# New sort keys for attention work, and fp32 logit products for the last units, in a fused attention and mixture-of-experts kernel

## The chip, the cores and the metric

The kernel runs on one core of a Trainium2 chip. The metric is the device time of one execution in microseconds. Engines are called PE or TensorE (matrix products), DVE or VectorE, ACT or ScalarE, POOL or GpSimd, and SP, which issues most of the DMAs; each works off its own instructions in the order in which the program gives them.

## The reference

Inputs are q, k and v of 8 batches x 8 heads x 576 rows x 64, a gate of 512 x 8, and the weights of 8 experts. Per batch and head:

```
q_d, k_d, v_d = means over groups of 4 rows               # 144 rows
out_up = repeat(softmax(q_d k_d^T / 8) v_d, 4)             # attention over groups
out_local = softmax(where(|i - j| < 4, q k^T / 8, -1e9)) v # a band of 7 keys
x = (out_up + out_local), as 4608 tokens x 512
logits = x @ w_gate                                        # 4608 x 8
# all (token, expert) pairs in order of falling logit; each token goes to the first
# expert that has room; an expert holds 4608 / 8 = 576 tokens
out[token] = relu(x[token] @ w1[e]) @ w2[e]
```

All of it is computed in fp32 or in pairs of f16 parts (a high and a low part), since the order of the logits decides the experts.

## The kernel before, in words

The attention stage comes first, then a routing step for the first expert, then eight experts in turn, each beside the routing of the next. The change touches the attention stage alone.

Tokens are taken in 36 units of 128 (`u`), each made of four windows of 32 queries with 38 keys. A batch (`b`) is 4.5 units long. A unit goes through steps: `s0`, `s1` (local scores on PE, maximum and subtraction on DVE, exponential on ACT; `loc_s`), `t` (four transposes on PE, line 552, copied by ACT as `pt`, line 563), `v0`, `v1` (products with the v rows `vw`, line 574, and normalisation on DVE), `up`/`um`/`add` (the attention over groups is added: up to unit 26 from a product, on DVE; from unit 27 on loaded from DRAM and added by POOL, line 582), `st` (store to DRAM), `lt` (transposes, line 592, and conversion to f16 high parts on ACT, line 601, and low parts on DVE, line 602), `lm` (products with the gate, lines 617 and 620; the logits are written by line 622).

A batch needs fill work: `trw`, `trt` (transposes of its q and k, lines 327 and 340, each copied from PSUM to SBUF by ACT or DVE, `evac`: every fifth copy goes to DVE later on, every second one at first), `gsum`, `gsum_v` (sums over groups of four, lines 267 to 303, on POOL, for batch 0's k on DVE) and `down_s`, `down_t`, `down_v` (the attention over groups, lines 349 to 443).

The order is set by one list. Every step has a key in units of time of one unit, and the list is sorted by it:

```
for j, (name, lag) in enumerate(LOC.items()):
    at = u + lag
    if lag >= 2.0:
        at = u + 2.0 + (lag - 2.0) * (1.0 - CE * max(u - UE, 0)) + max(E0 - u * E1, 0.0)
    if u >= UL:
        at += {"t": TX, "v": VX, "v0": VX, "v1": VX}.get(name, 0.0)
work.sort(key=lambda z: z[:3])
```

Fill work is spread over a stretch (`TW` and `TWS` for the transposes, `DW` and `DWS` for the attention over groups), loads have keys of their own (`LD1` for batch 1, `NEXT` for the later ones, `VWT0` up to unit `UV` and `VWT` from there for `vw`), and so have batch 0's sums (`SUM0`). The engines get their instructions in this order. Some parts of a step are put off by a number of TensorE steps: the exponential of the local scores by `FL` of them, or until `t` of its unit needs it, the low part of `lt` by `FT`. A load whose key is above `PACE0` is paced: SP issues it when the DVE instruction that stands last before it in the list is done; SP takes its DMAs in order.

Units from `UF` on convert the transposed rows as fp32 (line 597) and take four fp32 products instead of eight f16 ones (line 613); before, `UF` is 36, so no unit does.

Of the kernel before, what the change touches and what calls it, by code (L numbers as in the profile page):

```python
# [37 lines left out]
LU = 2  # L38
LA = 3
LT = 5  # L40
NEXT = (("q0", 1.46), ("q1", 1.71), ("k0", 2.06), ("k1", 2.37), ("t", 2.77), ("q2", 3.07), ("q3", 3.38), ("k2", 3.68), ("k3", 4.31),
        ("v0", 4.61), ("v1", 4.77), ("v2", 4.92), ("v3", 5.11), ("w", 5.13))
VWS = 0.22
PACE0 = 0.6
FD = 4
FN = 1
FH = 2
FL = 4
FT = 3
PEL = ("s0", "s1", "t", "v0", "v1", "lt", "lm")  # L50
TW = (0.23, 2.44)
DW = (0.15, 1.9)
DWS = {0: (1.95, 3.56), 7: (0.89, 2.3)}
LOC = {'up': 2.07, 'um': 4.42, 'st': 4.6, 't': 1.194, 'lm': 8.317, 's0': 0.33, 's1': 0.331, 'lt': 5.433, 'v0': 1.842, 'v1': 1.843, 'add': 4.425}
GS1 = ''
GS0 = 'k'
GW = 2
# [11 lines left out]
SETUP = {24: 0, 35: 25}  # L69
SPACE = 0.365  # L70
GS = 32.0
VWT = 1.219
VWT0 = 1.68
UV = 5
T0 = (-0.12, 0.19)
LD0 = (-1.79, -1.53, -1.57, -0.7, 0.51)
LD1 = (-0.99, -0.95, -0.9, -0.89, -0.88, -0.6, -0.55, -0.3, -0.25, 0.2, 0.4, 0.6, 0.8, 2.0)
TWS = {1: (1.54, 2.38)}
E0 = 0.72
E1 = 0.55  # L80
UE = 33
CE = 0.14
UF = 36
UL = 30
TX = 0.0
VX = 0.0
NWARM = 13
EV0 = (0,1)
EN0 = 24
TB = 3  # L90
SUM0 = (0.65, 1.38, 1.73)


def key0(w):
# [7 lines left out]
class Attention:  # L102
# [413 lines left out]
    def loc_s(self, u, g):  # L516
# [18 lines left out]
        if g == 0:  # L535
# [7 lines left out]
                                mx[..., None].to_broadcast([128, 2, 4, KW]), op=OP.subtract)  # L543
        self.after(FL, lambda: nc.scalar.activation(t[:, :, :KW], t[:, :, :KW], AF.Exp, scale=0.125), ("l", u))

# [41 lines left out]
    def log_t(self, u):  # L587
# [6 lines left out]
        pf = p.rearrange("p c t -> p (c t)")  # L594
        if u >= UF:
            xt = xt.rearrange("p a c t -> p (a c t)").bitcast(F32)
# [9 lines left out]
    def log_m(self, u):  # L606
# [3 lines left out]
        l = self.ps.tile([128, 2, E], F32, name="g", bufs=NG)  # L610
        if u >= UF:
            for c in range(4):
# [33 lines left out]
    def run(self, after, ready):  # L646
# [14 lines left out]
        for b in range(B):  # L661
# [5 lines left out]
            else:  # L667
                spread(-2.0, -1.0, t[:2] + t[3:])
                spread(T0[0], T0[1], t[2:3])
                for c in range(2):  # L670
                    for w in "kq":
                        other.append((SUM0[c], lambda w=w, c=c: self.gsum(0, w, 2 * c)))
                other.append((SUM0[2], lambda: self.gsum_v(0)))
            dw = DWS.get(b, DW)
            spread(u0 + dw[0], u0 + dw[1], self.down(b))
            end.append(u0 + dw[1])
            if b + 1 < B:
                for i, (w, at) in enumerate(NEXT):
                    at = max(up + at + (SH1 if b == 1 else 0), -1.0) if b else LD1[i]
                    f = lambda b=b, w=w: self.load_nat(b + 1, w[0], int(w[1]) if w[1:] else None)  # L680
# [18 lines left out]
        for u in range(NT):  # L699
            if u > 1:  # L700
                for c in range(4):
                    at = max(u - (VWT0 if u < UV else VWT) + VWS * c, u - 3.999 + LOC["v0"])
                    f = lambda u=u, c=c: self.load_vw(u, (c,))
                    work.append((at, 0, 0, (lambda f=f: self.paced(f)) if at > PACE0 else f, False))
# [7 lines that stand above are left out]
                if name == "up":  # L712
# [779 lines left out]
```

## Time and profile before

| | us |
|---|---|
| median of three runs | 710.55 |
| lowest and highest | 707.21, 711.26 |
| the profiled execution | 709.79 |
| its span | 708.1 |
| PE busy | 649.8 (92%) |
| DVE busy | 533.6 (75%) |
| ACT busy | 337.7 (48%) |
| POOL busy | 232.7 (33%) |

The span is the stretch from the first to the last instruction of the profiled execution; all places below are counted in us from its start. The profile gives for each engine the time in which an instruction ran, and for each idle stretch what seems to have ended it. [...]

### The profile page before, as it was taken

The page shows a single profiled execution, that of the slowest core. Times are in us where ns is not written, and L with a number is a line of the kernel's source. Part 1 is how long each engine was busy: PE and PEld are TensorE (multiplying, and loading weights), DVE is VectorE, ACT ScalarE, POOL GpSimd, SP SyncE. Part 2 cuts the span into 40 slices and gives each one's busy share as a digit, 9 for nine tenths or more (in the row PEclk, how much of TensorE's full clock was granted, in tenths as well). Part 3 has the DMA queues.
Part 4 walks back from the last instruction along what each step waited for, and adds up shares of the span by engine and source line. Part 5 has one row for each costly group of instructions (what it writes and reads, how often), then busy time and mean ns, then how long its engine had stood idle before and what let it go on. Part 6 is the DMA issues. An engine that isn't in the chain of part 4 may idle for free.

```text
span 708.1 us, 21934 instructions
## 1 busy us (share of the span) xinstructions
PE 649.8 (92%) x8938; PEld 451.0 (64%) x8938; DVE 533.6 (75%) x1562; ACT 337.7 (48%) x650; POOL 232.7 (33%) x303
## 2 busy tenths in 40 slices
PE   6888999889999845999999999999999999999994
PEld 4667878778787733774574575575674674755741
DVE  5798889987989977887889697797797876634500
ACT  4567778787785521532532443443444424424410
POOL 4865374644737420402402303204104106202011
PEclk9899999999999975999999999999999999999997
DMA  9967859777785632605507617638348269814001
GB/s 263 245 157 218 227 159 245 205 205 202 197 238 160 192 117 89 218 1 181 192 1 283 157 43 269 129 116 229 95 183 204 55 233 198 313 35 100 1 31 38
DMA packets 132157, 113.73 MB, mean 161 GB/s; under 512 B 81240, under 2 KB 109912, under 8 KB 132056
## 3 DMA queue, kind: packets, MB, share of 16 engines
q1 hardware_dynamic: 124760, 90.76, 45.0%
q0 software_dynamic: 6432, 20.98, 9.5%
q8 instruction: 71, 1.16, 0.7%
q10 hardware_dynamic: 864, 0.58, 0.3%
q14 instruction: 30, 0.25, 0.1%
HBM read 85.74 MB, written 19.46 MB: 149 GB/s over the span
## 4 chain that ended last, share of the span: by engine, by line
PE 45%; DVE 22%; issue 17%; ACT 5%; DMA 5%; POOL 4%; SPq 1%; ACTq 0%; POOLq 0%; DVEq 0%
PE pH L1279 13%; PE pX L1320 11%; PE g L574 3%; PE pR L871 2%; DVE wl L1202 2%; PE g L327 2%; POOL out_dram L1330 2%; DVE x L453 2%; PE g L552 2%; PE g L592 2%; PE s L532 1%; DVE qt L311 1%; POOL xg L1217 1%; PE g L407 1%; PE pH L1186 1%
## 5 line engine op out<-in xcount | busy, mean ns | idle before, releaser
L1279 PE MATMUL pH<-xt,wh 128*128 128x256 f16 (+1 forms) x1024 | 191.3, 286 | 1.2 <-ACT xt L1238 0.5
L1320 PE MATMUL pX<-wh,ht 128*128 128x512 f16 (+1 forms) x640 | 178.0, 379 | 0.0
L1279 PE MATMUL pH<-xt,wl 128*128 128x320 f16 (+1 forms) x512 | 144.6, 286 | 0.0
L1320 PEld LDWEIGHTS <-ht 128*128 128x128 f16 (+1 forms) x960 | 82.6, 100 | 93.9 <-issue 3.8
L1320 PE MATMUL pX<-wl,ht 128*128 128x512 f16 (+1 forms) x320 | 117.6, 379 | 0.0
L1279 PEld LDWEIGHTS <-wh 128*128 128x128 f16 x1024 | 97.5, 98 | 30.2 <-issue 5.7
L1330 POOL DMA_INDIRECT out_dram<-y,idx x40 | 43.0, 1074 | 177.8 <-ACT y L1327 153.5
L1303 ACT ACTIVATE ht<-pH 128x512 f16<-128x512 f32 (+1 forms) x128 | 45.5, 407 | 112.5 <-PE pH L1279 112.5
L1202 DVE SCALAR_TENSOR_TENSOR wl<-nat,wh 128x512 f16<-128x512 f32 x128 | 83.5, 687 | 14.9 <-ACT wh L1200 8.3
L1327 ACT ACTIVATE y<-pX 128x512 f32<-128x512 f32 (+1 forms) x40 | 23.8, 594 | 103.4 <-PE pX L1320 54.3
L1306 DVE SCALAR_TENSOR_TENSOR ht<-pH,ht 128x512 f16<-128x512 f32 (+1 forms) x128 | 52.3, 450 | 24.4 <-ACT ht L1303 23.9
L1200 ACT ACTIVATE wh<-nat 128x1024 f16<-128x1024 f32 x64 | 67.3, 1053 | 4.1 <-DMA nat<-in_moe_w_dram 4.1
L1217 POOL DMA_INDIRECT xg<-x_dram,idx x40 | 42.5, 1062 | 61.9 <-DVE used L1100 33.4
L1279 PEld LDWEIGHTS <-wl 128*128 128x128 f16 x512 | 49.9, 98 | 12.7 <-issue 0.8
L563 ACT COPY pt<-g 64x512 f32<-64x512 f32 x72 | 41.8, 581 | 28.8 <-PE g L552 27.8
L574 PE MATMUL g<-vw,pt 128*64 128x65 f32 x1152 | 45.5, 229 | 5.6 <-issue 2.7
L574 PEld LDWEIGHTS g<-vw,pt 128*64 128x64 f32 x1152 | 39.6, 142 | 12.7 <-issue 6.6
L327 PE MATMUL g<-ident,nat 128*128 128x128 f32 x256 | 40.4, 283 | 3.9 <-DMA nat<-in_q_dram 3.3
L313 ACT COPY kt<-g 64x512 f32<-64x512 f32 (+1 forms) x60 | 38.3, 639 | 6.2 <-PE g L327 5.2
L1246 DVE SCALAR_TENSOR_TENSOR xs<-xg,xs 128x512 f16<-128x512 f32 (+1 forms) x30 | 20.3, 688 | 26.8 <-ACT xs L1245 15.7
L1019 POOL MEMSET f<- 128x1 bf16 x8 | 0.8, 106 | 116.3 <-DVE sumf L925 44.2
L300 POOL TENSOR_TENSOR gtmp<-kt 128x576 f32<-128x576 f32 x14 | 16.1, 1147 | 61.4 <-ACT kt L313 43.6
(221 smaller groups left out, 1153.0 us busy)
## 6 DMA issues: line engine op xcount, KB each, us to landing
nat<-in_moe_w_dram SPq DMA_DIRECT2D x28, 1024.0 KB
vw<-in_v_dram SPq DMA_DIRECT2D x136, 78.0 KB
x_dram<-x SPq DMA_DIRECT2D x36, 256.0 KB
nat<-in_q_dram SPq DMA_DIRECT2D x32, 256.0 KB
nat<-in_k_dram SPq DMA_DIRECT2D x32, 256.0 KB
nat<-in_v_dram SPq DMA_DIRECT2D x28, 256.0 KB
up<-up_dram SPq DMA_DIRECT2D x9, 256.0 KB
nat<-in_moe_w_dram SPq DMA_DIRECT2D x4, 512.0 KB
```

The costliest lines, as they stand in the source:

```text
L313: self.nc.scalar.copy(out, in_)
L327: nc.tensor.transpose(p[:, a, :, fp], src[:, 4 * hh + 2 * a + s, 2 * fp:2 * fp + 2].rearrange("p f d -> p (f d)"), self.ident)
L563: self.nc.scalar.copy(out, in_)
L574: nc.tensor.matmul(o[64 * i:64 * i + 64, 65 * h:65 * h + 65], pt[:, 2 * (h % 2) + i, 2 * g + h // 2].rearrange("p b q -> p (b q)"), self.v ...
L1200: nc.scalar.activation(hi, r, AF.Copy, scale=sc)
L1202: nc.vector.scalar_tensor_tensor(lo[:, a:a + LOP], r[:, a:a + LOP], sc, hi[:, a:a + LOP], op0=OP.mult, op1=OP.subtract)
L1217: self.fetched = nc.gpsimd.indirect_dma_start(out=xg[:n], out_offset=None, in_=self.x, in_offset=bass.IndirectOffsetOnAxis(ap=idx[:n, c:c ...
L1279: mm = nc.tensor.matmul(p[:, s, :s1 - s0], w[d][a][:, 128 * f:128 * f + 128], xt[:, b, d, s0:s1], start=j == 0, stop=j == len(seq) - 1)
L1303: last = nc.scalar.activation(hi, q, AF.Relu)
L1306: low = nc.vector.scalar_tensor_tensor(lo, q, 0.0, hi, op0=OP.max, op1=OP.subtract)
L1320: mm = nc.tensor.matmul(p[o:o + m], ht[:, f, h0:h0 + m], w[4 + f // 2][b][:, 512 * (f % 2):512 * (f % 2) + 512], start=j < parts, stop=j > ...
L1330: i = nc.gpsimd.indirect_dma_start(out=self.out, in_=y[:n], in_offset=None, out_offset=bass.IndirectOffsetOnAxis(ap=idx[:n, c:c + 1], axis=0))
```

## The change

Only constants change. `SUM0` gives the places of batch 0's sums (first half, second half, v), `LOC['t']` that of the local transposes, `FL` the delay of the exponential, `VX` with `UL` an offset of the local values of the last units, `CE` a stretch of the last units' steps, `UF` the first unit with fp32 logits; the others are places of loads.

```
-NEXT = (... ("k1", 2.37), ("t", 2.77), ("q2", 3.07), ... ("v2", 4.92), ("v3", 5.11), ("w", 5.13))
+NEXT = (... ("k1", 2.37), ("t", 3.25), ("q2", 3.07), ... ("v2", 4.92), ("v3", 5.49), ("w", 4.9))
-FL = 4
+FL = 5
-LOC = {..., 't': 1.194, 'lm': 8.317, ...}
+LOC = {..., 't': 1.298, 'lm': 8.317, ...}
-VWT = 1.219
+VWT = 1.154
-UV = 5
+UV = 6
-LD1 = (-0.99, -0.95, -0.9, -0.89, -0.88, -0.6, -0.55, -0.3, -0.25, 0.2, 0.4, 0.6, 0.8, 2.0)
+LD1 = (-0.99, -0.95, -0.9, -0.89, -0.88, -0.87, -0.77, -0.11, -0.25, 0.2, 0.4, 0.6, 0.8, 2.0)
-CE = 0.14
-UF = 36
-UL = 30
+CE = -0.021
+UF = 34
+UL = 31
-VX = 0.0
+VX = -0.052
-SUM0 = (0.65, 1.38, 1.73)
+SUM0 = (0.53, 1.65, 1.67)
```

The step that `UF` switches, in `log_m`:

```
        if u >= UF:
            for c in range(4):
                nc.tensor.matmul(l[:, 0], xt[:, c], self.wgf[:, c], start=c == 0, stop=c == 3)
            nc.vector.tensor_copy(self.lg[:, u], l[:, 0])
            return
```

## Rows read from the trace of the kernel before

**Rows 1.** Busy time of the engines in a stretch, with granted clock and DMA share.

```profile
120.00:140.00 20.00, 17.98 (x550) 15.41 (x542) 18.96 (x56) 13.62 (x26) 13.79 (x21) 1.00 0.78 204
```

**Rows 2.** Groups by line, PE, 60 to 220 us: busy, mean ns, idle before, releasers.

```profile
L552 PE MATMUL g<-ident,sw 128*128 128x128 f32 x100 | 15.8, 281 | 8.0 <-ACT sw L544 7.8
```

**Rows 3.** Waits over the whole span: us in total, times, longest.

```profile
PEld g L327 <- DMA nat<-in_q_dram: 4.4, 4, 2.2
```

**Rows 4.** Timeline of batch 3's last transposes: start, us, engine, line, [idle before].

```profile
96.78 1.19 ACT L563 COPY pt<-g 64x512 f32<-64x512 f32 x2
96.81 0.66 PE L592 MATMUL g<-ident,x 128*128 128x128 f32 x4
...
97.99 1.27 ACT L313 COPY kt<-g 64x512 f32<-64x512 f32 x2
98.02 1.22 PE L574 MATMUL g<-vw,pt 128*64 128x65 f32 x32 [0.55 <-ACT pt L563]
...
99.66 0.15 DVE L450 TENSOR_SCALAR den<-g 128x4 f32<-128x4 f32 x1
...
100.29 0.66 PE L552 MATMUL g<-ident,sw 128*128 128x128 f32 x4 [1.04 <-ACT sw L544]
```

**Rows 5.** Timeline behind the last transposes of batch 2, then of batch 4.

```profile
62.61 1.17 ACT L563 COPY pt<-g 64x512 f32<-64x512 f32 x2
...
64.41 1.83 PE L574 MATMUL g<-vw,pt 128*64 128x65 f32 x32
...
67.92 0.66 PE L552 MATMUL g<-ident,sw 128*128 128x128 f32 x4 [1.68 <-ACT sw L544]
...
72.56 0.66 PE L552 MATMUL g<-ident,sw 128*128 128x128 f32 x4
...
127.81 0.66 PE L552 MATMUL g<-ident,sw 128*128 128x128 f32 x4 [1.05 <-ACT sw L544]
...
131.20 0.66 PE L552 MATMUL g<-ident,sw 128*128 128x128 f32 x4
```

**Rows 6.** Busy time and granted clock (third from the end) behind these waits.

```profile
70.00:72.00 2.00, 2.00 (x28) 1.67 (x28) 1.57 (x5) 0.94 (x2) 1.81 (x6) 0.50 0.63 196
...
128.00:130.00 2.00, 2.00 (x89) 1.77 (x88) 1.88 (x8) 1.16 (x2) 1.82 (x3) 1.00 0.88 277
```

**Rows 7.** Timeline of the first units.

```profile
18.87 0.76 DVE L300 TENSOR_TENSOR gtmp<-kt 128x576 f32<-128x576 f32 x1 [0.68 <-POOL qdt L303]
...
20.26 1.15 POOL L300 TENSOR_TENSOR gtmp<-qt 128x576 f32<-128x576 f32 x1 [1.43 <-DVE kdt L303]
...
21.49 0.40 POOL L303 TENSOR_TENSOR qd<-gtmp 128x128 f32<-128x128 f32 x1
...
22.31 1.39 DVE L311 COPY kt<-g 64x512 f32<-64x512 f32 x2 [2.19 <-PE g L327]
...
26.88 1.01 PE L356 MATMUL g<-kdt,qd 64*128 64x144 f32 x12
...
36.64 0.36 ACT L313 COPY ptd<-g 128x256 f32<-128x256 f32 x1
...
36.80 0.66 PE L552 MATMUL g<-ident,sw 128*128 128x128 f32 x4 [0.53 <-ACT sw L544]
```

**Rows 8.** Timeline of the last units.

```profile
253.53 2.54 POOL L582 TENSOR_TENSOR x<-x,up 128x512 f32<-128x512 f32 x2 [3.32 <-PE g L592]
...
256.12 0.42 PEld L592 LDWEIGHTS g<-ident,x 128*128 128x128 f32 x4 [0.53 <-POOL x L582]
256.12 0.66 PE L592 MATMUL g<-ident,x 128*128 128x128 f32 x4 [0.43 <-POOL x L582]
...
257.63 0.69 DVE L602 SCALAR_TENSOR_TENSOR xt<-g,xt 128x512 f16<-128x512 f32 x1 [0.24 <-ACT xt L601]
...
258.38 0.27 PE L620 MATMUL g<-wg,xt 128*128 128x8 f16 x4 [0.45 <-DVE xt L602]
```

**Rows 9.** Line 362: duration ns min/median/max, first and last start, form.

```profile
L362 PEld LDWEIGHTS g<-kdt,qdz x32: 186/190/192, 31.0 to 227.1; 128*128 128x128 f32 x32
```

More of the change, by code (lines that the diff above doesn't have):

```diff
@@ L40 @@
 LT = 5
-NEXT = (("q0", 1.46), ("q1", 1.71), ("k0", 2.06), ("k1", 2.37), ("t", 2.77), ("q2", 3.07), ("q3", 3.38), ("k2", 3.68), ("k3", 4.31),
-        ("v0", 4.61), ("v1", 4.77), ("v2", 4.92), ("v3", 5.11), ("w", 5.13))
+NEXT = (("q0", 1.46), ("q1", 1.71), ("k0", 2.06), ("k1", 2.37), ("t", 3.25), ("q2", 3.07), ("q3", 3.38), ("k2", 3.68), ("k3", 4.31),
+        ("v0", 4.61), ("v1", 4.77), ("v2", 4.92), ("v3", 5.49), ("w", 4.9))
 VWS = 0.22
@@ L53 @@
 DWS = {0: (1.95, 3.56), 7: (0.89, 2.3)}
-LOC = {'up': 2.07, 'um': 4.42, 'st': 4.6, 't': 1.194, 'lm': 8.317, 's0': 0.33, 's1': 0.331, 'lt': 5.433, 'v0': 1.842, 'v1': 1.843, 'add': 4.425}
+LOC = {'up': 2.07, 'um': 4.42, 'st': 4.6, 't': 1.298, 'lm': 8.317, 's0': 0.33, 's1': 0.331, 'lt': 5.433, 'v0': 1.842, 'v1': 1.843, 'add': 4.425}
 GS1 = ''
```

## The prediction

> **What bounds the kernel now.** I read the busy time by stretches first, then the idle time by line, then the timeline around the places that the change moves. The change touches the attention stage only, which ends near 259 us; the routing and the eight experts behind it keep their order and should only shift. In an attention stretch TensorE and VectorE are both nearly full: in 20 us VectorE is busy for 18.96 and TensorE for 17.98 [rows 1]. Whatever saves time must therefore shorten one of these two or remove a wait of both; work that moves between other work of a full engine saves nothing. The one large wait of TensorE in the middle is that of the local transposes (`t`, L552) for their exponential: 7.8 us between 60 and 220 us [rows 2]. It comes once a batch, at the first unit after the last transposes of the next batch's q and k; there TensorE waits for ACT, ACT for VectorE's subtraction, and VectorE is working through its queue. Waits for a loaded q tile are 4.4 us, in four times [rows 3], and I find them all at the start. Behind the last unit a chain through GpSimd's sums, transposes, conversion and logits ends the stage [rows 8].
>
> **Reading the change as order.** The constants are only sort keys, so I sorted the work by them before and after and compared each engine's order. Most of what moves crosses nothing on its own engine: in units without fill work `t` goes from lag 1.194 to 1.298 and meets neither another TensorE step nor an ACT one, and the exponential, due one piece later, still stands right ahead of it on ACT. What really changes places is this.
>
> **1. `t` behind a transpose, three times a batch (b = 2 to 7).** The transposes of the next batch lie 0.23, 1.212 and 2.194 behind the same whole unit, and 0.194 becomes 0.298: `t` goes behind the first q one, the second k one and the last k one. The first two (12 swaps) lie among down work, far ahead of the products that need `t`: 0; ends 1 us either way, two waits like the 0.53 us that a `t` of the first units shows [rows 7]. The third is close to its reader. In batch 3 ACT copies `pt` from 96.78 to 97.97, then k's for 1.27; the value products wait for `pt` until 98.02 [rows 4]. After, k's copy goes ahead: 96.78 + 1.27 + 1.19 for `pt` = 99.24, so they start at about 99.3, 1.27 later. They end at 99.3 + 1.22 = 100.5 rather than 99.24; the next `t` starts at 100.29 now, because its exponential ends then, so TensorE loses 0.2. VectorE's next normalisation starts at 99.66 behind other work and would have to wait some 0.4 [rows 4]. Lower end 0 (swallowed by TensorE's later waits), upper end 1.27; I take 0.25, as the next `t` moves by 0.2. Batches 4 and 6 show the same pattern, three in all: 3 x 0.25 = +0.75, ends 0 and 3.8. In batch 5 the last k copy falls to VectorE, which takes every fifth one, so ACT's order stays: 0. In batch 7 the products don't wait: 0.
>
> Batch 2 differs. There `pt` is copied from 62.61 and the products run from 64.41, and `t` then waits 1.68 us, up to 67.92 [rows 5]. With k's copy ahead of `pt` (62.61 + 1.27 + 1.17) the products start at about 65.1, and the 1.68 us break into 0.7 ahead of them and 1.0 behind; `t` itself stays at 67.92, as VectorE sets it. What may change is the clock. [...] From this `t` to the next it is 72.56 - 67.92 = 4.64 us in batch 2 and 131.20 - 127.81 = 3.39 in batch 4 [rows 5]: a fall costs about 1.25 us. I take -1.2 for batch 2; ends 0 and -1.25.
>
> **2. The first units.** The second half of batch 0's sums goes behind two transposes. On VectorE it fills a gap either way. On GpSimd the q part, which waits for the k part, started at 20.26 [rows 7]. After, VectorE is done with the k copy at 22.31 + 1.39 = 23.7 and needs some 1.3 for the k part (first of two steps 0.76); the q part starts at 25.1 and has the third head pair written (21.49 + 0.40 - 20.26 = 1.63) at 26.7. The first scores over groups started at 26.88 [rows 7]: just met. All of GpSimd's work behind it moves by 4.8 us, up to the next gap in its work; who reads that has some 5 us now. 0, with an upper end of 1. Unit 2's `t` goes behind the values over groups of batch 0, which need the copy that ends at 36.64 + 0.36 = 37.00; `t` started at 36.80 after a wait of 0.53 [rows 7], so TensorE starts again 0.2 later: +0.2, ends -0.5 and 0.5.
>
> **3. Loads.** q's second half of batch 1 goes ahead of unit 1's v rows, one v load of each later unit is issued behind the norm instead of ahead of it, and the load of the short tail 0.48 unit later. The bytes are the same, the q and k loads that TensorE waited for go first as before [rows 3], the others have a unit or more to spare: 0, within 1 us, since the loads share one queue.
>
> **4. The tail.** The sums of the last two units on GpSimd start at 253.53 after a wait of 3.32 us and end at 256.07 [rows 8]. The view puts the wait down to transposes that these sums don't read; I take it for the arrival of the rows they add. Small shifts ahead of it may so be swallowed. Behind them, before: transposes at 256.12, a conversion, at 257.63 VectorE's low part, at 258.38 the last four products, done at 258.65 [rows 8]: 1.02 us from the conversion. After, the low part goes (for units 34 and 35), and each unit takes four fp32 products, which the other fp32 products of the trace carry out as two instructions each: eight weight loads of 128x128 fp32. One is 0.42 / 4 = 0.105 us in the last transposes and 0.19 as a single one [rows 8, 9], so 0.84 to 1.5 us a unit. Unit 33's eight f16 products (two groups that overlap, 0.27 for one; 0.4 together) and unit 34's come first in TensorE's queue, from 256.8: 256.8 + 0.4 + 2 x 0.84 = 258.9, against 258.65: +0.2. Ends -0.4 (unit 34's hidden behind the conversion) and +1.5 (the dearer load). So I don't expect the fp32 products to shorten the chain that VectorE's step leaves.
>
> **Sum.** +0.75 - 1.2 + 0.2 + 0 + 0.2 = -0.05 us against the profiled execution's 709.79 us (span 708.1 and 1.7 around it): 709.7 us. The median of the runs shown, 710.55, lies 0.8 above that execution.
>
> **Rivals.** *New falls of the clock (slower).* In batches 3, 4 and 6 the wait ahead of the value products grows from 0.55 us to 1.8, from 97.47 to 99.3 [rows 4], in one piece, more than the 1.68 us of batch 2 behind which the clock fell [rows 5, 6]. Three falls cost 3 x 1.25 = 3.75: 709.7 + 3.75 = 713.4, and 714.6 if batch 2 keeps its own. It decides from about 1.7 us of wait. For it speaks that length; against it that TensorE's idle sum around the products, 0.55 + 1.04, hardly grows and the clock stood at that. [...] Chance 0.18.
>
> *The waits for the exponential go (faster).* If a transpose in front of `t`, and the other load order, let VectorE run ahead, then the 7.8 us [rows 2] shrink and the falls behind them with them, one in batch 2 and one more in batch 5. Half of the waits and both falls: 3.9 + 2.5 = 6.4, less the 1 us paid elsewhere: 709.8 - 5.4 = 704.4. For it: this is the largest wait there is. Against it: VectorE's queue sets it and loses nothing but two conversions at the very end. Chance 0.24.
>
> *The moves cancel:* that is the forecast's own case, 0.58; its own range is 707 to 712.
>
> **How the numbers follow.** A measurement can tell about 0.5%, 3.55 us, from no change. Faster by more 0.24, within 0.58, slower by more 0.18. The range reaches into both rivals: 705 to 713.4.
>
> **What would show it.** In batches 3, 4 and 6 the value products should start 1.2 to 1.3 us later, with the granted clock still 1.00 behind; a clock of 0.5 there is the slower rival. In batch 2 the wait at `t` should be about 1.0 us and the clock 1.00. The q sums of batch 0 should begin on GpSimd at about 25 us. Ahead of the routing, the last logits should be written at 258.5 to 259.5. The prediction is wrong if the waits for the exponential fall by more than 3 us in sum, if group scores wait for GpSimd between 26 and 45 us, or if the last sums on GpSimd start more than 1.5 us away from 253.5 without a like shift of what comes before.

## The result and the profile after

The changed kernel takes 716.67 us, the median of 4 runs (715.98 to 722.61), against 710.39 for the kernel before, measured beside it (4 runs, 707.21 to 711.26): a ratio of 1.0107, with a 95% interval of 1.0068 to 1.0146. It is slower by 1.1%; I had forecast 709.7 and a range up to 713.4.

The profiled execution takes 716.21 us with a span of 714.5. All that is lost is lost in the attention stage. Its last logits are written at 265.18 + 0.17 = 265.35 us; in the kernel before the last four products end at 258.65 [rows 8], and the logits are written at 258.69 + 0.18 = 258.87, 6.5 earlier. From there to the end of the span it is 449.2 us in both.

TensorE's groups between 60 and 220 us, by line; the columns are as in [rows 2]:

```profile
L574 PE MATMUL g<-vw,pt 128*64 128x65 f32 x738 | 30.7, 236 | 7.4 <-ACT pt L563 6.8 <-issue 0.3 <-ACT kt L313 0.2
...
L552 PE MATMUL g<-ident,sw 128*128 128x128 f32 x92 | 15.4, 294 | 3.6 <-ACT sw L544 3.6
```

The line of the value products in the kernel before:

```profile
L574 PE MATMUL g<-vw,pt 128*64 128x65 f32 x786 | 31.3, 231 | 2.2 <-ACT pt L563 1.7 <-issue 0.3
```

The wait of the local transposes for their exponential fell from 7.8 us [rows 2] to 3.6; the value products, in front of them, now wait 6.8 us for `pt` instead of 1.7. The wait moved one step up the chain: the idle time before both lines together is 11.0 us, before it was 10.2. A fall of the first wait by more than 3 us was one of my signs of being wrong. It came, but not for the reason of the faster rival, and nothing was gained by it. The timeline of batch 3 shows how; it answers to [rows 4]:

```profile
97.53 1.23 ACT L313 COPY kt<-g 64x512 f32<-64x512 f32 x2
...
97.56 0.65 PE L592 MATMUL g<-ident,x 128*128 128x128 f32 x4
...
98.79 1.18 ACT L563 COPY pt<-g 64x512 f32<-64x512 f32 x2
...
100.00 0.60 ACT L601 ACTIVATE xt<-g 128x512 f16<-128x512 f32 x1
...
100.03 1.22 PE L574 MATMUL g<-vw,pt 128*64 128x65 f32 x32 [1.81 <-ACT pt L563]
...
100.82 0.16 DVE L450 TENSOR_SCALAR den<-g 128x4 f32<-128x4 f32 x1 [0.33 <-PE g L574]
...
101.18 0.95 PE L552 MATMUL g<-ident,sw 128*128 128x128 f32 x4
```

k's last copy goes first, then `pt`, then the products: one wait of 1.81 us where 0.55 and 1.04 us stood. Batches 4 and 6 have the same line at 129.04 and 193.91 us, with 1.82 us each. Busy time and granted clock (third from the end) behind the three places:

```profile
98.00:100.00 2.00, 0.22 (x2) 0.00 (x0) 1.94 (x6) 1.92 (x4) 0.93 (x1) 1.00 0.78 208
100.00:102.00 2.00, 1.97 (x38) 1.84 (x39) 1.53 (x7) 0.94 (x2) 1.88 (x3) 0.85 0.63 134
102.00:104.00 2.00, 2.00 (x84) 1.32 (x82) 1.69 (x5) 1.16 (x2) 1.89 (x4) 0.50 0.68 209
...
130.00:132.00 2.00, 2.00 (x28) 1.88 (x25) 1.32 (x6) 0.00 (x0) 1.84 (x3) 0.50 0.93 296
...
194.00:196.00 2.00, 2.00 (x33) 1.88 (x34) 0.90 (x4) 0.83 (x2) 1.84 (x3) 0.50 0.72 198
```

TensorE did next to nothing from 98 to 100 us and was then granted 0.50 of its full clock; 0.50 and 1.00 are the only levels in the traces of the kernel before and the changed one. These are the falls of my slower rival, in all three batches of this profile.

The first units. GpSimd's q sums of batch 0 start at 24.24 us, close to the 25 that I forecast, and all of its work behind them is later; at 43 us its sums of v meet VectorE's low parts. Timeline:

```profile
42.84 1.27 POOL L272 TENSOR_TENSOR gtv<-nat 128x512 f32<-128x512 f32 x1
...
42.97 2.83 DVE L471 SCALAR_TENSOR_TENSOR u<-xu,u 64x512 f16<-64x512 f32 x2
...
44.19 1.06 POOL L273 TENSOR_TENSOR vd<-gtv 128x256 f32<-128x256 f32 x1
...
45.32 1.60 POOL L272 TENSOR_TENSOR gtv<-nat 128x512 f32<-128x512 f32 x1
45.83 1.17 DVE L471 SCALAR_TENSOR_TENSOR yh<-yu,yh 128x64 f16<-128x64 f32 x1
...
47.85 0.41 PE L327 MATMUL g<-ident,nat 128*128 128x128 f32 x2 [2.20 <-issue]
```

The two steps of L471 in the kernel before:

```profile
43.01 1.55 DVE L471 SCALAR_TENSOR_TENSOR u<-xu,u 64x512 f16<-64x512 f32 x2
...
44.59 0.23 DVE L471 SCALAR_TENSOR_TENSOR yh<-yu,yh 128x64 f16<-128x64 f32 x1
```

They took 1.55 and 0.23 us there; now they take 2.83 and 1.17, and GpSimd's own steps 1.60 and 1.06 instead of 1.27 and 0.73. The transposes behind stand still for 2.20 us; unit 4's `t` starts 2.6 later than before.

Batch 5's group work, around the first transpose of batch 6. Timeline of the changed kernel, then of the kernel before:

```profile
170.94 0.66 PE L327 MATMUL g<-ident,nat 128*128 128x128 f32 x4
...
171.43 0.60 PE L552 MATMUL g<-ident,sw 128*128 128x128 f32 x4
...
172.22 0.76 PE L532 MATMUL s<-kt,qt 64*32 64x38 f32 x64
...
172.80 1.27 ACT L313 COPY qt<-g 64x512 f32<-64x512 f32 x2 [3.45 <-POOL gtv L277]
...
174.09 1.19 ACT L563 COPY pt<-g 64x512 f32<-64x512 f32 x2
...
175.30 0.52 ACT L375 ACTIVATE sd<-sd 128x384 f32<-128x384 f32 x1
...
180.52 0.55 PE L391 MATMUL g<-ident,sd 128*128 128x128 f32 x3 [1.00 <-ACT sd L375]
```

```profile
165.62 0.65 PE L552 MATMUL g<-ident,sw 128*128 128x128 f32 x4
...
166.36 1.19 ACT L563 COPY pt<-g 64x512 f32<-64x512 f32 x2 [2.48 <-PE g L552]
...
166.90 0.76 PE L532 MATMUL s<-kt,qt 64*32 64x38 f32 x64
...
167.57 1.27 ACT L313 COPY qt<-g 64x512 f32<-64x512 f32 x2
...
168.73 0.51 ACT L375 ACTIVATE sd<-sd 128x384 f32<-128x384 f32 x1
...
173.94 0.55 PE L391 MATMUL g<-ident,sd 128*128 128x128 f32 x3 [0.71 <-ACT sd L375]
```

Before, `pt` is copied 0.74 us after its transposes start, ahead of q's copy. After, q's copy stands in front on ACT and waits 3.45 us, although its transposes were done at 171.6. It starts 0.58 us after the local scores (172.80 - 172.22). Two of unit 22's four windows still read batch 4's q, and with two buffers that is the tile that batch 6's q overwrites. The view names GpSimd as the releaser; in this and seven other profiles with this swap the copy starts 0.57 to 0.58 us behind the scores' start, so I take these for what it waits for. `pt` comes 2.66 us after its transposes instead of 0.74, and batch 5's group exponentials come later with it: the last of their transposes (L391) starts 9.09 us behind `t` (180.52 - 171.43) instead of 8.32 (173.94 - 165.62).

The tail, answering to [rows 8]:

```profile
262.52 0.66 PE L592 MATMUL g<-ident,x 128*128 128x128 f32 x4 [0.46 <-POOL x L582]
...
263.21 0.60 ACT L597 ACTIVATE xt<-g 128x512 f32<-128x512 f32 x1 [0.70 <-PE g L592]
263.22 1.93 PE L613 MATMUL g<-wgf,xt 128*128 128x8 f32 x16
...
265.18 0.17 DVE L614 COPY lg<-g 128x8 f32<-128x8 f32 x1 [0.73 <-PE g L613]
```

From the end of the last conversion to the last logits it is 265.35 - 263.81 = 1.54 us; before, from 257.60 to 258.87, it was 1.27: +0.3, where I took +0.2.

### The profile page after: what moved, and what is told of

It reads as the page before. It is cut to its first block, busy times and chain, and to the rows that moved or that the text cites. A ratio compares the mean times of both kernels' runs of the same rounds, so it can differ in the third digit from the quotient of the medians.

```text
span 714.5 us, 21898 instructions
## 1 busy us (share of the span) xinstructions
PE 654.1 (92%) x8938; PEld 455.1 (64%) x8938; DVE 535.0 (75%) x1560; ACT 338.7 (47%) x650; POOL 231.9 (32%) x303
## 4 chain that ended last, share of the span: by engine, by line
PE 45%; DVE 19%; issue 17%; DMA 6%; ACT 6%; POOL 4%; SPq 1%; ACTq 0%; POOLq 0%; DVEq 0%
PE pX L1320 13%; PE pH L1279 12%; PE g L574 3%; PE g L327 2%; PE pR L871 2%; DVE wl L1202 2%; POOL xg L1217 2%; POOL out_dram L1330 2%; PE g L552 2%; PE s L532 2%; DMA xg<-x_dram,idx 1%; ACT kt L313 1%; DVE x L453 1%; PE g L592 1%; ACT pt L563 1%
## 5 line engine op out<-in xcount | busy, mean ns | idle before, releaser
L1279 PEld LDWEIGHTS <-wl 128*128 128x128 f16 x512 | 49.9, 98 | 12.7 <-issue 0.8
L574 PEld LDWEIGHTS g<-vw,pt 128*64 128x64 f32 x1152 | 41.0, 146 | 17.8 <-ACT pt L563 10.2
L327 PEld LDWEIGHTS g<-ident,nat 128*128 128x128 f32 x256 | 28.7, 144 | 10.4 <-issue 2.6
```

The lines of the kernel that those rows point to most:

```text
L327: nc.tensor.transpose(p[:, a, :, fp], src[:, 4 * hh + 2 * a + s, 2 * fp:2 * fp + 2].rearrange("p f d -> p (f d)"), self.ident)
L574: nc.tensor.matmul(o[64 * i:64 * i + 64, 65 * h:65 * h + 65], pt[:, 2 * (h % 2) + i, 2 * g + h // 2].rearrange("p b q -> p (b q)"), self.v ...
L1279: mm = nc.tensor.matmul(p[:, s, :s1 - s0], w[d][a][:, 128 * f:128 * f + 128], xt[:, b, d, s0:s1], start=j == 0, stop=j == len(seq) - 1)
```

## The experiments

**Undoing the two suspects, and doing one alone.**

```diff
 e1: -SUM0 = (0.53, 1.65, 1.67)   +SUM0 = (0.65, 1.38, 1.73)   (changed kernel)
 e2: -LOC 't': 1.298              +LOC 't': 1.194               (changed kernel)
 e4: -LOC 't': 1.194              +LOC 't': 1.298               (kernel before)
```

> The changed kernel with SUM0 as before. Theory (two causes: GpSimd's later sums hold up VectorE's low parts of batch 0, +2.4 us; k's last copy ahead of pt makes three waits of 1.8 us with a fall of the clock, +5 us): the 2.4 us go, so about 714.3 us, last logits written at about 263.0 instead of 265.35; the three low parts of batch 0 last 0.7/0.7/1.1 and 0.23 us each again; the waits for pt of 1.8 us in batches 3, 4 and 6 and the granted clock of 0.5 behind them stay. Rival (loads, the later exponential or unit 2's swap cost the first units): 716.7 us, last logits at 265.3, and VectorE's low parts as long as in the changed kernel.

> The changed kernel with the local transposes' lag as before (1.194). Theory (two causes): waits for pt in batches 3, 4 and 6 are 0.55 us again and the clock stays at 1.00 there; batch 2 has its wait of 1.68 us and its fall of the clock back (+1.1): 716.7 - 5.2 + 1.1 = 712.6 us, last logits at 261.3. Rival (the local values' loads, now issued behind a norm, or the later exponential make the waits): waits and falls stay, over 715.5 us.

> The kernel before with only the local transposes' lag changed to 1.298. Theory (the lag alone makes the three falls of the clock): batches 3, 4 and 6 wait 1.8 us for pt, granted clock 0.5 behind each, batch 2 loses its fall: 710.4 + 5.2 - 1.1 = 714.5 us, last logits at about 263. Rival (the lag does no harm without the other constants): 710.4 us or less, clock 1.00 in batches 3, 4 and 6.

Measured against the kernel before: e1 1.0106 (1.0067 to 1.0145), e2 1.0043 (1.0013 to 1.0073), e4 1.0061 (1.0030 to 1.0092). The lag alone costs, and undoing it gives back some 0.6%, so its theory holds for the time. It does not hold for batch 2: e2's profile has no fall of the clock between 27 and 258 us, where I expected batch 2's fall back, and e4 has one there, where I expected it to go. Undoing the sums gave nothing in time, though VectorE's low parts took no longer than before again (at most 1.10 and 0.23 us a step); that theory fell as far as the time goes. In e4's profile the clock fell in batch 3 but not in 4 and 6, behind waits of 1.60 and 1.68 us.

**Keeping the clock up.** Seven matmuls of ones where TensorE waits:

```diff
 e8, changed kernel, in loc_v, and e9, kernel before, the same in loc_t for u in (6, 20):
+        if g == 0 and u in (10, 14, 23):
+            for _ in range(7):
+                nc.tensor.matmul(o, self.wm, self.wm[:, None].to_broadcast([128, 4, 128]), start=True, stop=True)
```

> The changed kernel with seven matmuls of ones (128x128 by 512, bf16, some 1.5 us) put ahead of the value products of units 10, 14 and 23, where TensorE waits 1.8 us for pt; what they write is overwritten. Theory (it is the clock behind the wait, not the wait, that costs): the products start when they did, the granted clock stays at 1.00 behind all three, and 4 to 5 us go: 712 us, last logits at about 261. Rival (the products' later start costs, through VectorE's next norm): the clock stays up but less than 1.5 us go, over 715 us.

> The kernel before with seven matmuls of ones (some 1.5 us) ahead of the local transposes of units 6 and 20, where TensorE waits 1.7 and 2.1 us for the exponential and the granted clock falls behind. What they write is overwritten. If the clock is what costs: clock 1.00 at 68 to 74 and 160 to 166 us, 2 to 2.5 us less, 707.5 us. If VectorE's queue sets these stretches: the clock stays up, less than 1 us less.

e8 took 1.0124 (1.0086 to 1.0162), e9 1.0009 (0.9976 to 1.0041). The timeline of e8 in batch 3:

```profile
97.88 1.67 PE L575 MATMUL g<-wm 128*128 128x512 bf16 x7
...
99.87 1.22 PE L578 MATMUL g<-vw,pt 128*64 128x65 f32 x32 [0.32 <-ACT pt L564]
```

The products start where they would, the clock stays at 1.00 in batches 3 and 6, and in e9 it stays up from 28 to 258 us. In e8 new falls begin in the windows from 132 and from 252 us on; ahead of the first of them TensorE waits 1.66 us, up to 132.21, for VectorE's subtraction. Neither kernel got faster: keeping the clock up at chosen places did not buy back the time.

**Parts that don't add up.**

```diff
 e3: changed kernel with 't': 1.194 and the old SUM0
 e7: kernel before with 't': 1.2            (passes only k's last transpose)
 f2: kernel before, 1.298 for all units but (5, 10, 14, 19, 23, 28)   (the other two swaps)
```

> The changed kernel with both the local transposes' lag (1.194) and SUM0 as before; what stays of the change are loads, the exponential one piece later, unit-2 swap and the tail. With the lag alone undone it took 712.5 (before: 709.9). Theory (the sums' new place holds up VectorE in batch 0, 1 to 2.4 us): 710.5 us, unit 4's transposes at 53.6 instead of 54.8. Rival (loads, exponential or tail cost the 2.6 us): 712.5 us.

> The kernel before with the local transposes' lag at 1.2: they go only behind k's last transpose, so that only k's last copy goes ahead of pt. The lag of 1.298 alone (all three swaps) cost 3.4 us in the median. Theory (k's last copy does it): 712.5 to 713.5 us, waits of 1.6 to 1.8 us for pt in batches 3, 4 and 6; the 1.00 us wait at unit 22 for the group exponentials (177 us) isn't there. Rival (the first two swaps, among the group work, cost as much): 710.5 to 711 us.

> The complement: the kernel before with the lag 1.298 but for the six units whose local transposes would pass k's last transpose (5, 10, 14, 19, 23, 28). Theory (k's last copy costs): the 1.00 us wait at 177 us for the group exponentials of batch 5 with some 1.2 us behind it is all that is left, 711 us; waits for pt in batches 3, 4 and 6 stay at 0.55 us. Rival (the first two swaps): 712.5 to 713.5 us.

e3 took 1.0070 (1.0035 to 1.0105), e7 1.0075 (1.0047 to 1.0103), f2 1.0049 (1.0020 to 1.0078). The medians, 715.7, 716.0 and 714.0 us, lie above both readings that I had written down for each. Both kinds of swaps cost, but together (e4, 1.0061) not more than one of them; and e3, with less of the change in it than e2 (1.0043), was no faster. For q's copy the profiles tell the swaps apart: from unit 21's `t` to unit 22's it is 10.13 us in f2, 8.93 in e7 and 8.92 in the kernel before. For the whole times something besides the moved steps had to be in them.

**Nothing moved but the place.** 18 or 9 tiny matmuls (8 columns) where TensorE waits 2.04 us for a q tile of batch 1:

```diff
 in trw (n0: no edit; n1: PAD 18, n2: PAD 9; n3: changed kernel, PAD 18)
+        if (b, which, hh, s) == (1, "q", 0, 0):
+            for _ in range(PAD):
+                nc.tensor.matmul(p.rearrange("p a i f -> p (a i f)")[:, :8], self.wm, self.wm[:, :8], start=True, stop=True)
```

> The kernel before, unchanged, in the place of a changed one. Seven kernels that each undo or do a part of the change took 711 to 718 us against 709.9, and their parts don't add up. If the comparison itself leans (a kernel that runs in the second place is slower), this one takes 712 us or more; if not, 709 to 711 us.

> The kernel before with 18 tiny matmuls (36 instructions of TensorE, 8 columns each, some 2 us) where TensorE waits 2.04 us for the first q tile of batch 1; nothing else moves in any engine's order. Theory (the moved steps cost): the time stays, 709 to 711 us. Rival (where TensorE's instructions fall in its stream of code, loaded in pieces of 16 KB during the run, moves stalls and falls of the clock, and any edit pays for that): 712 us or more, stalls for nothing that the profile shows in other places than 42, 48, 155, 242 and 247 us.

> The same with 9 tiny matmuls (18 instructions, some 1 us). Theory (the moved steps cost): 709 to 711 us. Rival (place of the code): another time than with 18, either side of it, and by more than 1.5 us away from 709.9 in one of the two.

> The changed kernel with the 18 tiny matmuls at the same place. Theory (the moved steps cost): 716 to 718 us as without them, waits of 1.8 us for pt in batches 3, 4 and 6 in place. Rival (place of the code): away from 716.7 by 2 us or more.

n0 took 0.9991 (0.9972 to 1.0010), so the kernel before takes the same time in the place of a changed one. n1 took 1.0047 (1.0022 to 1.0072) and n2 1.0026 (1.0003 to 1.0049): matmuls that do nothing cost 3.3 and 1.8 us. n3 took 1.0095 (1.0068 to 1.0121), like the changed kernel. Of the three places tried, the kernel before does best at its own. Why the sum changes is open; the first units are a little later, and stalls that nothing in the profile releases come elsewhere (the last section says what they go with). The same kernel shows them in different places too. n0 (the kernel before once more) stops inside one group of four transposes, where the profile of the kernel before that I predicted from has no such line:

```profile
137.78 0.28 PE L592 MATMUL g<-ident,x 128*128 128x128 f32 x1
...
140.27 0.49 PE L592 MATMUL g<-ident,x 128*128 128x128 f32 x3 [2.21 <-issue]
```

**The lag and the rest at two more places.** To take the place out of the comparison, I ran the lag alone, the rest alone (loads, sums, exponential, tail) and both, with 9 and 18 tiny matmuls.

> The changed kernel with 9 tiny matmuls ahead of batch 1's first transposes. So far: before 710.2, with 9 of them 711.9, with 18 714.8; changed 716.7, with 18 717.9. Theory (the moved steps cost, whatever the place of the code): 5 to 7 us above before with 9, 717 to 719 us. Rival (before stands at a lucky place and any other is dearer): 712 to 715.5 us.

> The kernel before with the lag of the local transposes at 1.298 and 9 tiny matmuls. Without them the lag cost 3.4 us. Theory (the lag costs by itself): 715 us, 3 us or more above before with 9. Rival (lucky place): within 1.5 us of 711.9.

> The same lag with 18 tiny matmuls. Theory (the lag costs by itself): 718 us, 3 us or more above before with 18 (714.8). Rival (lucky place): within 1.5 us of 714.8.

> The changed kernel with the lag as before (loads, sums, exponential and tail stay changed) and 9 tiny matmuls. Without them it took 712.5, 2.6 above before. Theory (the rest costs 2 to 2.6 by itself, in the first units): 714 us. Rival (the rest costs nothing, and 712.5 is the loss of the lucky place): within 1.5 us of 711.9.

> The changed kernel with the lag as before and 18 tiny matmuls. Theory (the rest costs 2 to 2.6 us by itself): 717 us, against 714.8 of before with 18. Rival (the rest costs nothing): within 1.5 us of 714.8.

Ratios to the kernel before (half width of the 95% interval 0.002 to 0.004):

| tiny matmuls | neither | lag alone | rest alone | both |
|---|---|---|---|---|
| 0 | 0.9991 | 1.0061 | 1.0043 | 1.0107 |
| 9 | 1.0026 | 1.0084 | 1.0008 | 1.0071 |
| 18 | 1.0047 | 1.0103 | 1.0063 | 1.0095 |

The lag costs in each of six pairs (neither to lag, rest to both): 0.0070, 0.0058, 0.0056, 0.0064, 0.0063, 0.0032; mean 0.0057, or 4.1 us. The rest costs 0.0052, -0.0018, 0.0016, 0.0046, -0.0013, -0.0008: mean 0.0013, 0.9 us, with both signs. One difference by itself is known to some 0.004; it is the six together that show the lag's cost, and the rest's is not told from none. The theory of a costly rest fell (m4 and m5, at 711.5 and 715.0 us, are its rival's), and so did the rival that the lag only loses a lucky place (m2 and m3, at 714.9 and 717.9 us, are as their theory has them). m1, at 715.9 us, lies between its theory and its rival. The two means make 0.7% of the changed kernel's 1.07%; what is left belongs to its place and stays open.

The six pairs of profiles say where. The mean shift of `t` between pairs grows by 1.26 us from unit 10 to 13 (batch 3; 0.69 to 1.46), by 1.80 from 13 to 17 (batch 4; 0.50 to 2.51), by 1.18 from 21 to 22 (q's copy in front of `pt`; 1.13 to 1.21, the steadiest of all) and by 0.8 from 22 to 27 (batch 6; -0.9 to 2.1). It falls by 0.7 from 4 to 8 (batch 2). At the stage's end it is 3.6, near the 4.1 of the times. From unit 10 to 34, with the two further profiles (n0, and m6 below) seven against seven: TensorE's idle time in the timelines is 14.8 us against 12.7, the time at the lower clock, added up from windows of 2 us, 7.8 against 2.9, the length 154.7 against 150.3. Idle time gives 2.1 of the 4.4, of which 0.4 is stalls of over 0.4 us without a releaser (2.8 us against 2.4). By my estimate the lower clock gives at most 2.4: half of the 4.9 us by which the two times at a granted 0.50 differ, if TensorE was the limit in all of them. But the loss does not need it. In three of the pairs the time at the lower clock is the same without the lag and with it (before and e4 3.4 us, n2 and m2 6.8, n1 and m3 3.4), and this stretch is longer by 4.0, 4.0 and 3.6 us all the same. How the loss divides between waiting and the clock is not shown; e8 and e9, which kept the clock up where I put the matmuls and gained nothing, speak for the waiting.

The falls: behind the products of batches 3, 4 and 6 the clock fell in 9 of 21 places with the lag (batch 3 in 4 of 7 profiles) and in none of 21 without it. With the lag the wait for `pt` is 1.81 to 1.83 us in 15 of the 21, and all nine falls are among these; in the other six it is 1.68 us or less. Where it did not fall, batch 3 cost 0.5 (m6) and 0.7 us (n3, with a stall of 0.74 late in it), or 1.28 with a stall of 0.88 in it (m3); where it fell, 1.4 to 1.5. The windows of m3:

```profile
98.00:100.00 2.00, 2.00 (x57) 1.90 (x65) 1.53 (x7) 1.01 (x3) 1.84 (x4) 1.00 0.64 155
100.00:102.00 2.00, 2.00 (x82) 1.37 (x80) 1.97 (x6) 1.13 (x3) 1.92 (x4) 1.00 0.70 212
102.00:104.00 2.00, 1.12 (x32) 0.95 (x30) 0.80 (x3) 0.86 (x2) 1.85 (x4) 1.00 0.28 77
...
130.00:132.00 2.00, 0.00 (x0) 0.00 (x0) 0.00 (x0) 0.01 (x1) 1.77 (x7) 1.00 0.45 127
```

Its wait ahead of the products is 1.81 us long and the clock stays at 1.00. The last line is the other cost: from 130 to 132 us TensorE, VectorE and ACT all stand still, and TensorE goes on after 2.54 us without a releaser. Batch 4 has such a stall of 1.7 to 2.5 us in four of the seven profiles with the lag and in one of the seven without it (2.21, n0). Whether the lag brings them is open.

**The tail.**

```diff
 m6: -UF = 34   +UF = 36   (changed kernel)
```

> The changed kernel with the last two units' logits as f16 products with a low part, as before (UF 36). In the changed kernel 1.54 us pass from the end of the last conversion to the end of the last logits, before 1.27. Theory (the fp32 products cost 0.2 to 0.3 us): about 1.3 us from the conversion, the time 0.3 us lower, not to be told from 716.7. Rival (they cost as much as a wait on VectorE and more): over 1 us less.

m6 took 1.0057 (1.0033 to 1.0081); the interval overlaps the changed kernel's. The median, 714.4 us, is 2.2 less, which alone would speak for the rival; but in the profiles m6 is 3.9 us ahead already where GpSimd's last sum ends (258.59 against 262.47), so this gain does not come from the tail. In its timeline the last conversion ends at 259.94 and the logits are written at 261.49:

```profile
259.34 0.60 ACT L601 ACTIVATE xt<-g 128x512 f16<-128x512 f32 x1 [0.21 <-PE g L592]
...
261.03 0.26 PE L620 MATMUL g<-wg,xt 128*128 128x8 f16 x4 [0.76 <-DVE xt L602]
...
261.32 0.17 DVE L622 TENSOR_REDUCE lg<-g 128x8 f32<-128x16 f32 x1 [0.35 <-PE g L620]
```

That is 1.55 us, as much as the 1.54 with fp32 products; the 1.3 us that I expected are missed. From the end of GpSimd's last sum it is 2.90 (261.49 - 258.59), and 2.88 with the fp32 products (265.35 - 262.47). The two forms can't be told apart.

## Why the prediction was wrong

- **The step that failed is step 1, the local transposes behind another one.** I took +0.75 for three swaps with k's last copy, 0 for the other twelve and -1.2 for batch 2: -0.45. The lag costs +4.1 us by time and +3.6 by the profiles. Batches 3 and 4 together cost 3.1 and batch 6 some 0.8 (with both signs), against 0.25 each; batch 4 costs 1.8 also from before to e4, with neither a fall nor a stall in it; one of the "free" twelve cost 1.18 every time.
- **Why 0.25 was too little.** The working was right up to the products: k's copy holds `pt` back from 97.53 to 98.79, by 1.26 us, and the next `t` is hardly later. I had priced what that `t` lost, and not what VectorE lost, though I had seen it: its next norm starts behind the products and waits 0.33 us for them (the line at 100.82), close to my 0.4, which went into no sum. Without a fall batch 3 costs 0.5 to 0.7 (1.28 in m3, with a stall); where the clock falls it costs some 0.8 more.
- **Why 0 was wrong for q's copy.** I asked how far away the reader of `pt` was. I did not ask what the copy that goes in front of `pt` on ACT itself waits for: as I read its start times, the scores that still read the q tile it overwrites. All that is queued behind it on ACT waits with it.
- **The slower rival was right in kind, and not enough by itself.** I gave it 0.18 and 1.25 us a fall. The falls came, in 9 of 21 places; at batch 3's 0.8 us and 1.3 falls a profile they would be some 1 us of the 4 (an estimate). Its condition, about 1.7 us of wait, does not decide: 6 of the 15 waits of 1.81 us or more went without a fall. My argument against it (the idle sum hardly grows, 0.55 + 1.04 to 1.81) was true and did not help: one wait in one piece brings a fall now and then, two short ones with the products between them did not in any of the 21 places.
- **Batch 2 went as forecast in the profile, and that was luck in part.** The 1.68 us broke into 0.79 and 1.21, the clock stayed at 1.00 there, and the mean gain is 0.7 of the 1.2. Other profiles with the lag (e4, m1, m2) have a fall there all the same, and two of the seven without it (n0, e2) have none. The -1.2 took for granted a fall that the kernel before does not have in every execution. n0 is the same kernel, with the same wait; its timeline, and the window that answers to [rows 6]:

```profile
68.42 0.66 PE L552 MATMUL g<-ident,sw 128*128 128x128 f32 x4 [1.68 <-ACT sw L544]
...
72.04 0.66 PE L552 MATMUL g<-ident,sw 128*128 128x128 f32 x4 [0.36 <-ACT sw L544]
```

```profile
70.00:72.00 2.00, 1.68 (x37) 1.37 (x35) 1.97 (x5) 1.41 (x3) 1.85 (x6) 1.00 0.68 217
```

From this `t` to the next it is 3.62 us instead of 4.64, so the fall cost 1.0 there, where I had 1.25 from batch 4's stretch [rows 5, 6]. Still n0's span is 708.9 us, without any fall from 27 to 258 us, and the span of the profile that I predicted from is 708.1.

- **The first units**, priced 0 with an upper end of 1: the rest of the change makes unit 4's `t` 1.4 us later in the mean of six pairs. That was mostly the collision on VectorE: e1, with the old sums, has this `t` at 54.5 us instead of 56.1. My "some 5 us of slack" looked only at who reads GpSimd's sums, not at what runs beside them. It is mostly regained: the rest's 0.9 us, the loads that I priced at 0 with it, are within its scatter. Unit 2's `t` starts 1.4 us later where I took 0.2 (38.24 against 36.80); by unit 3 that is gone (44.23 against 44.05).
- **The tail** was right within 0.2 us.
- **Beyond the steps**, the kernel before stands at a place from which tiny matmuls alone took it 1.8 and 3.3 us away. My sum had no term for that, and the range of 8 us was too narrow for it on the upper side.

## What to carry to other kernels

When a step goes ahead of another on an engine, ask first what it waits for itself, and who stands behind it; the distance to the reader comes second. Price a later start by all engines that hang on it, not by the one that you follow. When a kernel is tuned to half a percent, run an edit that does nothing beside your change, and compare the change at several such places: single parts did not add up here, six pairs gave the lag's 4 us. And look at a second execution of the same kernel before a fall of the clock goes into a sum.

## What I had not expected of the hardware

- VectorE's step of line 471 (`u<-xu,u`) and GpSimd's sums both take longer where they overlap: VectorE's 1.55 us became 2.37 to 2.83 in all seven kernels with the new sums whose timelines I read, and GpSimd's 1.27 and 0.73 became 1.60 to 1.76 and 1.06. e3, with the old sums, has 1.55. In the kernel before the step met only two smaller sums (L277, L278), which took 0.80 and 0.65 us there and 0.46 and 0.32 in the changed kernel. The cause is not shown.
- A wait of TensorE of the same length was followed by the lower clock in some executions and not in others: in batch 3, with 1.81 or 1.82 us, in 4 of 7; in batch 2 of the kernel before, with 1.68 us, in one of two.
- Stalls of 0.5 to 2.5 us in TensorE's stream without a releaser, in other places from execution to execution. The profile has a queue of instruction transfers that run beside the kernel; the line on it is the same for the kernel before and the changed one:

```profile
q8 instruction: 71, 1.16, 0.7%
```

These are 71 pieces of 16.3 KB; with 17,876 instructions of TensorE (matmuls and weight loads) that is 252 for each piece. In the kernel before 43 of the 71, 61%, fall between 20 and 256 us, as do 10,736 of these instructions, 60%, so I take the pieces for TensorE's instructions. Most pass without a stall: between 20 and 256 us the 20 profiles have 855 such transfers and 95 stalls of over 0.4 us that the view puts down to nothing ("issue"). The stalls go with the transfers: 92 of the 95 end 1.0 to 1.7 us after a piece has landed, where 12% of moments picked at random would. That TensorE waits there for its instructions is how I read this; the profile names no releaser. In sum the stalls are 2.2 to 8.3 us a profile, 3.7 and 7.9 in two executions of the same kernel (before and n0), as much as the lag costs. Why one piece goes with a stall and another does not is open.
